# Keys and queries of the last three batches: turned by blocked loads and VectorE copies instead of TensorE

## The chip, the cores and the metric

The kernel runs on one core of a Trainium2 chip, as a single program in a single launch. The metric is the device time of one execution in microseconds, and less is better. Instructions stand in one queue for each engine and run there in that order: TensorE (PE; its weight loads are PEld) multiplies matrices into PSUM, VectorE (DVE) and ScalarE (ACT) work elementwise on SBUF and PSUM, GpSimd (POOL) masks, clears and takes maxima over partitions, and SyncE (SP) issues nearly all DMAs. An instruction waits at the head of its queue until what it needs is there, and what is queued behind it waits too.

## What is computed

Attention with decay over 4 batches, 8 heads, 576 tokens and a head size of 64, and after it two feed-forward layers over all 2304 tokens, everything in float32:

```python
scores = scale * np.matmul(q, k.transpose(0, 1, 3, 2))
log_f = np.log(np.clip(f, 0.0001, 1.0))
cum = np.cumsum(log_f, axis=-1)
scores = np.where(causal, -1e9, scores + cum[:, :, :, None] - cum[:, :, None, :])
attn = softmax(scores)                                 # over the keys
x = (attn @ v), heads side by side: [2304, 512]
h = x @ moe_w_in;    x = (np.maximum(h, 0) + alpha * np.minimum(h, 0)) @ moe_w_out
h = x @ moe2_w_in;   out = np.where(h >= 1, h, np.where(h <= -1, 0, (h + 1) ** 2 / 4)) @ moe2_w_out
```

`w_in` is 512 by 2048 and `w_out` 2048 by 512 in both layers.

## The kernel before

**Order.** The kernel is written as a list of tasks. `add(engine, duration, function, position, dependencies, ...)` puts one on the list, and `Order.emit` walks through time with the durations and latencies that the source states, takes for each engine the ready task with the lowest position, and calls its function, which records the instructions. That fixes each engine's queue when the program is built; the hardware then only follows it. `Ring` and `Buf` are the planner's buffers: a task that takes a new buffer waits until all users of its previous content are done. A change in one task's engine or stated duration therefore moves tasks all over the queues.

**Precision.** Large products are made of three matmuls: a float32 value is split into a leading part (`...hi`, a copy to the type float32r, on ScalarE) and a remainder (`...lo`, a subtraction, on VectorE), and the small by small product is left out.

**Stages.** The first batch's attention (`plain_pair`, the units `u < 2`) runs in about the first 100 us. The other three batches follow, 24 units of work: three batches, two row blocks each (256 rows, then 320), four head pairs each. Between their tasks stand those of the first feed-forward layer (`l1_slice`: twelve matmuls of 256 columns into `ps_h` in L1320, the activation in L1330 to L1343, and twelve into `ps_y` in L1359), in chunks of 256 tokens. From about 480 us on the rest of the first layer and the whole second layer follow.

**One unit of the last three batches** (L831 to L1197). `load_k` and `load_q` fetch the pair's keys and queries with `load_tok`: token on the partition, the two heads' 2 x 64 values beside each other in a row, 256 bytes a run, one DMA for each head and one more for the last 64 tokens of a block of 320. They land in a `raw` buffer (two of them, shared with V) and in `qr` (one). Scores need the head size on the partitions, so `ktr` (L881) and `qtr` (L918) turn them on TensorE, 128 tokens a matmul, into a PSUM buffer of the ring `s` (three buffers, which the scores use too). From there `khi` (L892) and `klo` (L895) write leading part and remainder of the keys to `kT`, on either half of the partitions for the pair's two heads, and `qhi`, `qhi2`, `qlo` (L928, L935, L931) do so for the queries; with that, one matmul of 128 partitions makes two of the three partial products. Keys of the first 256 tokens are kept in DRAM (`stash`, L905) and read again (`reload`, L871) for the second row block, so that it turns only the remaining 320, as three groups of 128 with padding.

Behind that come the score matmuls (L994), bias and mask (L1008, L545), the maximum over the keys (L1029, L1047, L1053), the exponential (L1069, L1074), its split (L1084, L1088), the product with V (L1108 to L1116), and the division by way of two small DMA trips (`gather`, `put`, `get`: L1154 to L1175).

## Time and profile before

| | us |
|---|---|
| median of three runs | 1004.61 |
| the three runs | 1007.04, 1003.51, 1004.61 |
| the profiled execution's own time | 1004.37 |
| its span | 1002.2 |
| TensorE busy in the span | 987.8 |
| VectorE busy | 773.3 |
| ScalarE busy | 628.6 |
| GpSimd busy | 111.1 |

The profile is that of one execution. The span runs from its first instruction to its last; 2.2 us lie outside of it. An engine's busy time counts from an instruction's start to its end, overlaps once. Instructions of one engine overlap: a matmul of 256 columns lasts 286 ns by the page, though the next one begins well before. What one takes in its queue is therefore read from one start to the next in the timeline. "L881" is a line of the kernel before. A releaser ("<- DVE g L1333") is what ended a wait.

### The profile page before, as it was taken

How to read it: one execution, taken by the hardware profiler on the slowest of the kernel's cores; microseconds unless marked ns; L12 is line 12 of the kernel's file. 1: busy time of each engine (PE TensorE's matmuls, PEld its weight loads, DVE VectorE, ACT ScalarE, POOL GpSimd, SP SyncE). 2: the span in 40 equal slices, each digit the busy share in tenths (PEclk: the TensorE clock that was granted, in tenths of full speed). 3: DMA queues.
4: the chain of work that ended last, by engine and by line, in shares of the span. 5: the costliest groups of instructions: out<-in, count | busy, mean ns of one | idle time of the engine just before them, and what ended most of it. 6: DMA issues, size and time to landing. Idle time of an engine off the chain costs nothing.

```text
span 1002.2 us, 19921 instructions
## 1 busy us (share of the span) xinstructions
PE 987.8 (99%) x6736; PEld 909.2 (91%) x6736; DVE 773.3 (77%) x1874; ACT 628.6 (63%) x1628; POOL 111.1 (11%) x222
## 2 busy tenths in 40 slices
...
GB/s 264 232 184 156 63 76 100 55 74 56 63 109 55 62 55 76 106 45 31 29 92 192 183 203 242 116 316 237 268 102 249 153 123 120 116 168 125 106 53 63
DMA packets 151940, 128.24 MB, mean 128 GB/s; under 512 B 83440, under 2 KB 122368, under 8 KB 151840
## 3 DMA queue, kind: packets, MB, share of 16 engines
...
q10 hardware_dynamic: 1088, 0.26, 0.1%
...
## 4 chain that ended last, share of the span: by engine, by line
PE 80%; DVE 10%; ACT 5%; issue 2%; DMA 2%; POOL 0%; SPq 0%; ACTq 0%; POOLq 0%
PE ps_z L1598 20%; PE ps_y L1359 12%; PE ps_h L1854 12%; PE ps_h L1320 12%; PE ps_h L1613 7%; PE ps_y L1447 4%; PE ps_h L1403 4%; PE ps_s L994 3%; DVE raw L1253 1%; PE ps_o L1108 1%; DVE raw L1258 1%; PE ps_o L1114 1%; PE ps_o L1116 1%; PE ps_o L1115 1%; DVE w L1272 1%
## 5 line engine op out<-in xcount | busy, mean ns | idle before, releaser
L1320 PE MATMUL ps_h<-x,w 128*128 128x256 f32 x1344 | 182.7, 286 | 1.9 <-DVE g L1333 1.6
L1359 PE MATMUL ps_y<-gg,w 128*128 128x256 f32 x1344 | 183.5, 286 | 0.0
L1320 PEld LDWEIGHTS ps_h<-x,w 128*128 128x128 f32 x1344 | 168.7, 190 | 3.0 <-DVE g L1333 2.4
L1359 PEld LDWEIGHTS ps_y<-gg,w 128*128 128x128 f32 x1344 | 168.9, 190 | 0.4
L1598 PE MATMUL ps_z<-w,gw 128*128 128x512 f32 x576 | 149.2, 393 | 0.0
L1854 PE MATMUL ps_h<-xc,wc 128*128 128x384 f32 x672 | 136.8, 338 | 0.0
L1854 PEld LDWEIGHTS ps_h<-xc,wc 128*128 128x128 f32 x672 | 121.2, 188 | 10.3
L1598 PEld LDWEIGHTS ps_z<-w,gw 128*128 128x128 f32 x576 | 106.7, 188 | 15.3
L1892 ACT ACTIVATE t<-t,half 128x384 f32<-128x384 f32 x64 | 39.5, 617 | 88.6 <-DVE t L1889 88.6
L1008 ACT ACTIVATE S<-ps_s,nb 128x320 f32<-128x320 f32 (+4 forms) x168 | 75.2, 453 | 10.0 <-PE ps_s L994 5.9
L1333 DVE SCALAR_TENSOR_TENSOR g<-g,calpha,ps_h 128x256 f32<-128x256 f32 x112 | 53.4, 478 | 30.8 <-ACT g L1330 29.2
L1598 PE MATMUL ps_z<-w,gg 128*128 128x512 f32 x288 | 72.4, 391 | 0.0
L994 PE MATMUL ps_s<-q,kT 128*128 128x320 f32 (+4 forms) x336 | 72.0, 297 | 0.4 <-ACT S L1008 0.3
L1901 ACT CAST gw<-t 128x384 fp32r<-128x384 f32 x64 | 32.6, 510 | 56.9 <-PE ps_z L1598 54.1
L1074 ACT ACTIVATE S<-S 128x320 f32<-128x320 f32 (+2 forms) x144 | 59.8, 425 | 11.0 <-DVE S L1069 10.6
L545 POOL TENSOR_SCALAR_AFFINE_SELECT S<-S 128x128 f32<-128x128 f32 (+1 forms) x120 | 41.4, 347 | 223.4 <-ACT S L1008 209.4
L1904 DVE TENSOR_TENSOR gw<-t,gw 128x384 fp32r<-128x384 f32 x64 | 35.5, 555 | 37.6 <-ACT gw L1901 36.8
L1053 POOL PARTITION_ALL_REDUCE pp<-pp x48 | 57.3, 1194 | 52.2 <-DVE pp L1047 22.9
L1330 ACT ACTIVATE g<-ps_h 128x256 f32<-128x256 f32 x112 | 42.8, 382 | 32.0 <-PE ps_h L1320 31.1
L1069 DVE TENSOR_TENSOR S<-pp,S 128x320 f32<-128x320 f32 (+4 forms) x168 | 57.9, 396 | 5.1 <-POOL pp L1053 4.7
L1598 PEld LDWEIGHTS ps_z<-w,gg 128*128 128x128 f32 x288 | 53.0, 188 | 9.5
L1342 DVE TENSOR_TENSOR gg<-g,gg 128x256 fp32r<-128x256 f32 x112 | 48.5, 433 | 12.7 <-ACT gg L1339 11.0
...
## 6 DMA issues: line engine op xcount, KB each, us to landing
wc<-wc SPq DMA_DIRECT2D x112, 256.0 KB, 2.7
...
```

The lines of the kernel that those rows point to most:

```text
L994: nc.tensor.matmul(out=sb.t[:, :m], lhsT=kt.t[:, kb * P:(kb + 1) * P], rhs=qt.t[:, t * NMAX + qo:t * NMAX + qo + m], start=(t == 0), stop= ...
L1008: nc.scalar.activation(out=Sb.t[:, so:so + m], in_=sb.t[:, :m], func=AF.Identity, bias=bias)
L1053: nc.gpsimd.partition_all_reduce(Mb.t[:, :n], Mx.t[:, :n], P, ReduceOp.max)
L1069: nc.vector.tensor_tensor(out=sl, in0=Mb.t[:, qo:qo + m], in1=sl, op=ALU.subtract)
L1074: nc.scalar.activation(out=Sb.t[:, :gn], in_=Sb.t[:, :gn], func=AF.Exp, scale=-SCALE)
L1320: nc.tensor.matmul(out=hb.t, lhsT=a[:, sl], rhs=b, start=(cc == 0 and t == 0), stop=(cc == NCC - 1 and t == 2))
L1333: nc.vector.scalar_tensor_tensor(out=gb.t, in0=gb.t, scalar=calpha[:, s:s + 1], in1=hb.t, op0=ALU.mult, op1=ALU.add)
L1342: nc.vector.tensor_tensor(out=gg.t[1], in0=gb.t, in1=gg.t[0].bitcast(F32), op=ALU.subtract)
L1359: nc.tensor.matmul(out=Y[c][e // 2][:, e % 2, :], lhsT=a[:, sl], rhs=b, start=(s == 0 and t == 0 and e % 2 == 0), stop=(s == NF - 1 and t ...
L1598: nc.tensor.matmul(out=zb.t, lhsT=a, rhs=b, start=(start and t == 0), stop=(stop and t == 2))
L1613: nc.tensor.matmul(out=hb.t, lhsT=a[:, sl], rhs=b, start=(cc == 0 and t == 0), stop=(cc == NCC - 1 and t == 2))
L1854: nc.tensor.matmul(out=hb.t[:, :m], lhsT=wb.t[:, z, sl], rhs=xb.t[y][:, cc, :], start=(begin and cc == 0 and t == 0), stop=(cc == 1 and t ...
```

## The change

A DMA places squares of 32 by 32 values. `load_blocks` makes four DMAs of a load, one for each head and each half of its 64 values; each fills 32 partitions. Token 32 i + r of a block goes to partition r of its quarter, and its 32 values to columns 32 i to 32 i + 31, so every run is 128 bytes. One copy of VectorE (`nc.vector.transpose`, a STREAM_TRANSPOSE over 128 partitions) then turns each square in its place, from the first 320 columns of the same buffer to the next 320, and what results is what `ktr` and `qtr` left in PSUM: head size on the partitions, tokens on the columns. The splits read it from there, from SBUF and not from PSUM. No PSUM buffer is taken, and the buffers of the loads are held until the last split is done. Keys are turned without padding, 320 columns for 384, and a memset of GpSimd (`kpad`) clears the 64 padded columns of `kT` in the units of 320 rows. `qr` grows from three blocks of 128 to five. The first batch's `plain_pair` and the loads of V stay as they were. The counts in the queues: 120 matmuls fewer, 48 copies more on VectorE, 24 memsets more on GpSimd, 192 DMAs of the new form for 120 of the old.

```diff
--- before.py
+++ after.py
@@ -218,6 +218,7 @@
     BH = B * H
     C1 = 256
     NRAW = 3
+    Z = 32
     NVAL = 10
     QA = 256
     RC = 3
@@ -457,11 +458,11 @@
         return A1[nm]
 
     RAW = [ap2.tile([P, NKB, 2, D], F32, name=f"raw{i}") for i in range(2)]
-    QR = [ap1.tile([P, 3, 2, D], F32, name="qr")]
+    QR = [ap1.tile([P, NKB, 2, D], F32, name="qr")]
     pads(V["vF"])
     for t in RAW:
         nc.gpsimd.memset(t[S % P:, NKB - 1], 0.0)
-    nc.gpsimd.memset(QR[0][S % P:, 2:], 0.0)
+    nc.gpsimd.memset(QR[0][S % P:, 2:3], 0.0)
     nc.gpsimd.memset(ph["qr"][S % P:, 2:], 0.0)
 
     def load_tok(dst, src, b, pr, t0, t1, eng=nc.sync):
@@ -477,6 +478,16 @@
                 out=dst[:r, n, :, :],
                 in_=src[b, 2 * pr:2 * pr + 2, t0 + n * P:t1, :].rearrange("h p d -> p h d"))
 
+
+    def load_blocks(dst, src, b, pr, t0, t1):
+        for j in range(2):
+            for x in range(0, D, Z):
+                nc.sync.dma_start(
+                    out=dst[j * D + x:j * D + x + Z, :t1 - t0].rearrange("r (i c) -> r i c", c=Z),
+                    in_=src[b, 2 * pr + j, t0:t1, x:x + Z].rearrange("(i r) c -> r i c", r=Z))
+
+    def flat(t):
+        return t.rearrange("p c j d -> p (c j d)")
 
     fb = {}
     fP = Buf(R["s"])
@@ -837,17 +848,17 @@
         k0 = QA if again else 0
 
         def load_k(kb_=kb_, b=b, pr=pr, nk=nk, k0=k0):
-            kb_.t = RAW[kb_.slot]
-            load_tok(kb_.t[:, k0 // P:], k, b, pr, k0, nk)
+            kb_.t = flat(RAW[kb_.slot])
+            load_blocks(kb_.t, k, b, pr, k0, nk)
 
         def load_q(qb_=qb_, b=b, pr=pr, q0=q0, q1=q1):
-            qb_.t = QR[0]
-            load_tok(qb_.t, q, b, pr, q0, q1)
-
-        T["lk"] = add("SP", tok_issue(k0, nk), load_k, p0 - 3, [last.get("lv"), last.get("lk")], new=[kb_],
-                      move=moved(2 * (nk - k0), 256))
+            qb_.t = flat(QR[0])
+            load_blocks(qb_.t, q, b, pr, q0, q1)
+
+        T["lk"] = add("SP", 1900, load_k, p0 - 3, [last.get("lv"), last.get("lk")], new=[kb_],
+                      move=moved(4 * (nk - k0), 128))
         last["lk"] = T["lk"]
-        last["lq"] = add("SP", tok_issue(q0, q1), load_q, p0 - 3, [last.get("lq")], new=[qb_], move=moved(2 * n, 256))
+        last["lq"] = add("SP", 1900, load_q, p0 - 3, [last.get("lq")], new=[qb_], move=moved(4 * n, 128))
 
         nsplit = sum(y[2] > PVF for y in blocks)
         nkp = -(-nk // P) * P
@@ -871,32 +882,30 @@
                     nc.sync.dma_start(out=k_of(j).bitcast(F32)[:, :QA], in_=kd[j])
 
                 kready[j].append(add("SP", 450, reload, p0 - 1, [owned[j]] + keep_st[b, pr], use=[kx[j]], move=moved(P, 4 * QA)))
-        for t0 in range(k0, nkp, KC):
-            t1 = min(nkp, t0 + KC)
-            pb = Buf(R["s"])
-
-            def ktr(pb=pb, kb_=kb_, t0=t0, t1=t1):
-                pb.t = ps_a.tile([P, 512], F32, tag=f"s{pb.slot}", name="pst")
-                for c in range(t0 // P, t1 // P):
-                    nc.tensor.transpose(
-                        pb.t[:, c * P - t0:(c + 1) * P - t0],
-                        kb_.t[:, c, :, :].rearrange("p j d -> p (j d)"), ident)
-
-            a = last["ktr"] = add("PE", 112 * (t1 - t0) // P, ktr, p0 - 1, [T["lk"], last.get("ktr"), owned[0]],
-                                  new=[pb], use=[kb_])
-            for j in range(2):
-                hr = slice(j * D, (j + 1) * D)
-                lr = slice(D - j * D, 2 * D - j * D)
-
-                def khi(j=j, hr=hr, pb=pb, t0=t0, t1=t1, k_of=k_of):
-                    nc.scalar.copy(out=k_of(j)[hr, t0:t1], in_=pb.t[hr, :t1 - t0])
-
-                def klo(j=j, hr=hr, lr=lr, pb=pb, t0=t0, t1=t1, k_of=k_of):
-                    nc.vector.tensor_tensor(out=k_of(j)[lr, t0:t1], in0=pb.t[hr, :t1 - t0],
-                                            in1=k_of(j)[hr, t0:t1].bitcast(F32), op=ALU.subtract)
-
-                h = add("ACT", act(t1 - t0), khi, p0 - 1 + j * JO, [a, owned[j]], use=[pb, kx[j]])
-                kready[j] += [h, add("DVE", dve(t1 - t0), klo, p0 - 1 + j * JO, [h], use=[pb, kx[j]])]
+        nl = nk - k0
+
+        def ktr(kb_=kb_, nl=nl):
+            nc.vector.transpose(out=kb_.t[:, GMAX:GMAX + nl], in_=kb_.t[:, :nl])
+
+        a = last["ktr"] = add("DVE", dve(nl), ktr, p0 - 1, [T["lk"], last.get("ktr")], use=[kb_])
+        for j in range(2):
+            hr = slice(j * D, (j + 1) * D)
+            lr = slice(D - j * D, 2 * D - j * D)
+            if nk < nkp:
+                def kpad(j=j, k_of=k_of, nk=nk, nkp=nkp):
+                    nc.gpsimd.memset(k_of(j).bitcast(F32)[:, nk:nkp], 0.0)
+
+                kready[j].append(add("POOL", 230, kpad, p0 - 1, [owned[j]], use=[kx[j]]))
+
+            def khi(j=j, hr=hr, kb_=kb_, nl=nl, k_of=k_of, k0=k0, nk=nk):
+                nc.scalar.copy(out=k_of(j)[hr, k0:nk], in_=kb_.t[hr, GMAX:GMAX + nl])
+
+            def klo(j=j, hr=hr, lr=lr, kb_=kb_, nl=nl, k_of=k_of, k0=k0, nk=nk):
+                nc.vector.tensor_tensor(out=k_of(j)[lr, k0:nk], in0=kb_.t[hr, GMAX:GMAX + nl],
+                                        in1=k_of(j)[hr, k0:nk].bitcast(F32), op=ALU.subtract)
+
+            h = add("ACT", act(nl), khi, p0 - 1 + j * JO, [a, owned[j]], use=[kb_, kx[j]])
+            kready[j] += [h, add("DVE", dve(nl), klo, p0 - 1 + j * JO, [h], use=[kb_, kx[j]])]
         if not again and nk == QA:
             kept[b, pr] = tc.dram_tile([2, P, QA], F32, name=f"kept{b}_{pr}")
             keep_st[b, pr] = []
@@ -907,36 +916,31 @@
                 keep_st[b, pr].append(add("SP", 450, stash, p0 + 1, kready[j], use=[kx[j]], move=moved(P, 4 * QA)))
 
         qready = [[], []]
-        pb = Buf(R["s"])
         qx = [Buf(R[f"qp{j}"]) for j in range(2)]
-        np_ = -(-n // P)
-
-        def qtr(pb=pb, qb_=qb_, np_=np_, qx=qx):
-            pb.t = ps_a.tile([P, 512], F32, tag=f"s{pb.slot}", name="pst")
-            qx[0].t = second("q0")
-            for c in range(np_):
-                nc.tensor.transpose(pb.t[:, c * P:(c + 1) * P], qb_.t[:, c].rearrange("p j d -> p (j d)"), ident)
+
+        def qtr(qb_=qb_, n=n):
+            nc.vector.transpose(out=qb_.t[:, GMAX:GMAX + n], in_=qb_.t[:, :n])
 
         pq = p0 + QOFF
-        a = add("PE", 112 * np_, qtr, pq, [last["lq"], last.get("qtr")] + plain_qk[0] + plain_qk[1], new=[pb, qx[0]], use=[qb_])
+        a = add("DVE", dve(n), qtr, pq, [last["lq"], last.get("qtr")] + plain_qk[0] + plain_qk[1], use=[qb_])
         last["qtr"] = a
         for j in range(2):
             hr = slice(j * D, (j + 1) * D)
 
-            def qhi(pb=pb, qb=qx[j], n=n, hr=hr, j=j):
+            def qhi(qb_=qb_, qb=qx[j], n=n, hr=hr, j=j):
                 qb.t = second(f"q{j}")
-                nc.scalar.copy(out=qb.t[hr, :n], in_=pb.t[hr, :n])
-
-            def qlo(pb=pb, qb=qx[j], n=n, hr=hr):
-                nc.vector.tensor_tensor(out=qb.t[hr, NMAX:NMAX + n], in0=pb.t[hr, :n], in1=qb.t[hr, :n].bitcast(F32),
+                nc.scalar.copy(out=qb.t[hr, :n], in_=qb_.t[hr, GMAX:GMAX + n])
+
+            def qlo(qb_=qb_, qb=qx[j], n=n, hr=hr):
+                nc.vector.tensor_tensor(out=qb.t[hr, NMAX:NMAX + n], in0=qb_.t[hr, GMAX:GMAX + n], in1=qb.t[hr, :n].bitcast(F32),
                                         op=ALU.subtract)
 
-            def qhi2(pb=pb, qb=qx[j], n=n, hr=hr, lr=slice(D - j * D, 2 * D - j * D)):
-                nc.scalar.copy(out=qb.t[lr, :n], in_=pb.t[hr, :n])
-
-            h = add("ACT", act(n), qhi, pq + j * JO, [a], new=[qx[j]] if j else [], use=[pb] if j else [pb, qx[j]])
-            h2 = add("ACT", act(n), qhi2, pq + j * JO, [a, h], use=[pb, qx[j]])
-            qready[j] = [h, h2, add("DVE", dve(n), qlo, pq + j * JO, [h], use=[pb, qx[j]])]
+            def qhi2(qb_=qb_, qb=qx[j], n=n, hr=hr, lr=slice(D - j * D, 2 * D - j * D)):
+                nc.scalar.copy(out=qb.t[lr, :n], in_=qb_.t[hr, GMAX:GMAX + n])
+
+            h = add("ACT", act(n), qhi, pq + j * JO, [a], new=[qx[j]], use=[qb_])
+            h2 = add("ACT", act(n), qhi2, pq + j * JO, [a, h], use=[qb_, qx[j]])
+            qready[j] = [h, h2, add("DVE", dve(n), qlo, pq + j * JO, [h], use=[qb_, qx[j]])]
 
         vb_ = Buf(R["raw"])
```

The order moves everywhere from the first of these units on. Three places, each from the kernel before and from the changed one, whose file is four lines longer by then (its L998 is L994, L1118 is L1114, L1324 is L1320, L1363 is L1359). TensorE's queue in the second batch, second row block, in the scores (`ps_s`) of a pair's second head; before:

```order
L1320 MATMUL ps_h<-x,w 128x256 x12
L994 MATMUL ps_s<-q_1911,kT 128x320 x2
L881 MATMUL pst<-ident,raw_163 128x128 x3
L994 MATMUL ps_s<-q_1911,kT 128x320 x2
L1114 MATMUL ps_o<-PH,vH 128x320
L1115 MATMUL ps_o<-PH,vL 128x320
L1116 MATMUL ps_o<-PL,vH 128x320
L994 MATMUL ps_s<-q_1911,kT 128x320 x2
```

The changed kernel at the scores of the second head there:

```order
L998 MATMUL ps_s<-q_1975,kT 128x320 x2
L1363 MATMUL ps_y_3415<-gg,w 128x256 x6
L1363 MATMUL ps_y_3416<-gg,w 128x256 x6
L998 MATMUL ps_s<-q_1975,kT 128x320 x2
L1118 MATMUL ps_o<-PH,vH 128x320
L1119 MATMUL ps_o<-PH,vL 128x320
L1120 MATMUL ps_o<-PL,vH 128x320
L998 MATMUL ps_s<-q_1975,kT 128x320 x2
```

The three transposing matmuls between two score matmuls are gone, and other wide groups stand between the scores.

VectorE's queue near the same place, where the remainders of keys (L895) and queries (L931) stand between passes of the softmax (L1047, L1088) and of the feed-forward layer (L1333, L1342); before:

```order
L1342 TENSOR_TENSOR gg<-g,gg 128x256
L1047 TENSOR_TENSOR pp<-S,pp 128x320
L895 TENSOR_TENSOR kT<-pst,kT 64x384
L1088 TENSOR_TENSOR PL<-S,PH 128x320
L931 TENSOR_TENSOR q_1858<-pst,q_1858 64x320
L1047 TENSOR_TENSOR pp<-S,pp 128x192
L1333 SCALAR_TENSOR_TENSOR g<-g,calpha,ps_h 128x256 x2
L895 TENSOR_TENSOR kT<-pst,kT 64x384
L1088 TENSOR_TENSOR PL<-S,PH 128x320
```

The changed kernel, with the copies (L888 for keys, L922 for queries) and the remainders (L904, L935):

```order
L1051 TENSOR_TENSOR pp<-S,pp 128x64
L1092 TENSOR_TENSOR PL<-S,PH 128x320
L888 STREAM_TRANSPOSE raw_164<-raw_164 128x320
L904 TENSOR_TENSOR kT<-raw_164,kT 64x320
L1073 TENSOR_TENSOR S<-pp,S 128x320
L1092 TENSOR_TENSOR PL<-S,PH 128x320
L1073 TENSOR_TENSOR S<-pp,S 128x320 x2
L1073 TENSOR_TENSOR S<-pp,S 128x192
L1073 TENSOR_TENSOR S<-pp,S 128x64
L1033 TENSOR_TENSOR pp<-S 128x320
L1337 SCALAR_TENSOR_TENSOR g<-g,calpha,ps_h 128x256
```

The copies are new rows in this queue, and the remainders read `raw` and `qr` where they read `pst`, the PSUM buffer.

SyncE's queue of the second batch, the key load of the first unit of 320 rows; before:

```order
L471 DMA raw_164<-in_k_dram 128x2x64 x2
L476 DMA raw_164<-in_k_dram 64x2x64
L1165 DMA m_2403<-spread_1_175 64x256
L1165 DMA pp<-spread_1_175 64x256
L471 DMA qr<-in_q_dram 128x2x64 x2
L476 DMA qr<-in_q_dram 64x2x64
```

The changed kernel at the same load:

```order
L485 DMA raw_164<-in_k_dram 32x10x32 x4
L485 DMA qr<-in_q_dram 32x10x32 x4
L1169 DMA m_2430<-spread_1_175 64x256
L1169 DMA pp<-spread_1_175 64x256
```

Three DMAs for the keys became four, and the four of the queries now stand right behind them, ahead of the small DMAs of the division (`m`, `pp`).

## Rows read from the trace of the kernel before

**Rows 1.** Page, part 1: busy us (share of span), instructions.

```profile
PE 987.8 (99%) x6736; PEld 909.2 (91%) x6736; DVE 773.3 (77%) x1874; ACT 628.6 (63%) x1628; POOL 111.1 (11%) x222
```

**Rows 2.** Windows: us; busy PE, PEld, DVE, ACT, POOL; PEclk, DMA share, GB/s.

```profile
100.00:480.00 380.00, 376.39 (x3102) 370.50 (x3100) 311.02 (x839) 315.37 (x925) 96.32 (x167) 1.00 0.28 69
...
520.00:600.00 80.00, 80.00 (x384) 67.48 (x383) 75.77 (x169) 47.01 (x108) 0.00 (x0) 1.00 0.65 196
...
600.00:1002.00 402.00, 398.45 (x1985) 351.52 (x1983) 273.14 (x588) 164.69 (x336) 0.00 (x0) 1.00 0.52 160
```

**Rows 3.** Timeline of TensorE: start us, us, line, operation, shape, count.

```profile
151.48 0.38 PE L881 MATMUL pst<-ident,raw 128*128 128x128 f32 x2
151.62 1.67 PE L1359 MATMUL ps_y<-gg,w 128*128 128x256 f32 x12
...
161.81 0.49 PE L881 MATMUL pst<-ident,raw 128*128 128x128 f32 x3
162.06 1.67 PE L1359 MATMUL ps_y<-gg,w 128*128 128x256 f32 x12
163.56 0.28 PE L1114 MATMUL ps_o<-PH,vH 128*128 128x256 f32 x1
...
163.92 1.59 PE L1359 MATMUL ps_y<-gg,w 128*128 128x256 f32 x12
165.34 0.38 PE L1108 MATMUL ps_o<-S,vF 128*128 128x128 f32 x2
```

**Rows 4.** One line, TensorE: ns min/median/max, first and last start.

```profile
L881 PE MATMUL pst<-ident,raw x60: 270/272/300, 110.2 to 460.3; 128*128 128x128 f32 x60
```

**Rows 5.** Timeline of VectorE: back-to-back passes.

```profile
160.28 0.71 DVE L1069 TENSOR_TENSOR S<-pp,S 128x256 f32<-128x256 f32 x2
160.91 0.28 DVE L1029 TENSOR_TENSOR pp<-S 128x128 f32<-128x128 f32 x1
...
179.22 0.48 DVE L931 TENSOR_TENSOR q<-pst,q 64x320 fp32r<-64x320 f32 x1
179.62 0.47 DVE L1088 TENSOR_TENSOR PL<-S,PH 128x320 fp32r<-128x320 f32 x1
```

**Rows 6.** Groups by shape, 100 to 480 us: busy us, mean ns.

```profile
L1069 DVE TENSOR_TENSOR S<-pp,S 128x320 f32<-128x320 f32 x69 | 30.2, 485 | 3.3 <-POOL pp L1053 3.0
L895 DVE TENSOR_TENSOR kT<-pst,kT 64x384 fp32r<-64x384 f32 x24 | 13.3, 556 | 2.3 <-ACT kT L892 1.5
L931 DVE TENSOR_TENSOR q<-pst,q 64x320 fp32r<-64x320 f32 x24 | 11.7, 486 | 1.5 <-ACT q L935 0.7 <-ACT q L928 0.4
...
L1245 DVE TENSOR_SCALAR val<-val 128x512 int32<-128x512 int32 x6 | 2.5, 425 | 0.0
...
L1339 ACT CAST gg<-g 128x256 fp32r<-128x256 f32 x88 | 35.7, 408 | 9.4 <-DVE g L1333 8.5
...
L928 ACT CAST q<-pst 64x256 fp32r<-64x256 f32 x24 | 8.8, 366 | 0.2
```

**Rows 7.** Two lines of VectorE, columns as in rows 4.

```profile
L1342 DVE TENSOR_TENSOR gg<-g,gg x112: 395/424/954, 45.2 to 526.4; 128x256 fp32r<-128x256 f32 x112
...
L931 DVE TENSOR_TENSOR q<-pst,q x48: 409/452/496, 122.9 to 467.0; 64x256 fp32r<-64x256 f32 x24, 64x320 fp32r<-64x320 f32 x24
```

**Rows 8.** TensorE waits, 100 to 480 us: total us, times, longest.

```profile
PE ps_h L1320 <- DVE g L1333: 1.6, 4, 0.6
PE pst L881 <- DMA raw<-in_k_dram: 0.5, 1, 0.5
```

**Rows 9.** SyncE timeline; DMA issues: KB each, median us to landing.

```profile
156.53 0.96 SPq L471 DMA_DIRECT2D raw<-in_k_dram  x2
157.54 0.64 SPq L476 DMA_DIRECT2D raw<-in_k_dram  x1
...
raw<-in_k_dram SPq DMA_DIRECT2D x54, 64.0 KB, 2.5
```

**Rows 10.** Groups by shape, 100 to 480 us, GpSimd.

```profile
L414 POOL MEMSET vH<- 128x192 f32 x1 | 0.3, 263 | 19.1 <-PE ps_o L746 19.1
```

## The prediction, made before the changed kernel had run

> **What bounds the kernel now.** I read the page first, for the engine that fills the span: TensorE is busy 987.8 us, 99% of the span [rows 1]. [...] Attention of the last three batches lies at about 100 to 480 us; there TensorE is busy 376.39 of 380.00 us, so it idles 3.6 us in all, while VectorE is busy 311.02 (idle 69.0), ScalarE 315.37 (idle 64.6) and GpSimd 96.32 [rows 2]. From 600 us to the end it idles 3.6 of 402 us. So the time is the length of TensorE's queue: a column less in it shortens the run, as long as no other engine makes it wait. Then I read the timeline of TensorE for what one of the removed groups takes from start to start, since its busy times overlap.
>
> **What goes from TensorE.** The 120 transposing matmuls stand in 48 groups: each of 24 units of work (three batches, two row blocks, four head pairs) has one group for keys and one for queries, of two matmuls in the 12 units of 256 rows and of three in the 12 of 320. That is 24 groups of two and 24 of three; the row of one line shows its half, x60 [rows 4]. A group of two holds the queue from 151.48 to 151.62, 0.14 us; one of three from 161.81 to 162.06, 0.25 us [rows 3]. So 24 x 0.14 + 24 x 0.25 = 9.4 us.
>
> There is a second part. The twelve matmuls of 256 columns behind a group of three take 162.06 to 163.56, 1.50 us, and behind a wide matmul 163.92 to 165.34, 1.42 us [rows 3]: what follows a narrow matmul starts its successor 0.08 us later. In the old order 102 matmuls of 256 columns or more stand behind one of 128 or fewer, 41 of them behind a transposing group; in the new order 64 do. So 38 x 0.08 = 3.0 us. Together TensorE's queue loses **12.4 us**, between 9.4 (if the second part stays) and 12.4.
>
> **What VectorE gets.** 48 transposing copies, 24 of 128x256 and 24 of 128x320. No row shows such a copy. Bounds: a pass of two inputs goes from start to start in 0.32 us at 256 columns (two from 160.28 to 160.91, 0.63) and 0.40 at 320 (179.22 to 179.62) [rows 5]. A pass with one input over 512 columns takes 425 ns [rows 6], against some 0.69 that two-input passes of that width would take at 556 ns per 384 plus 1.1 ns a column, so 0.6 of it: 0.20 and 0.25. Above, a copy that goes at half rate costs two passes, 0.64 and 0.80. So 24 x (0.20 + 0.25) = 10.8, 24 x (0.32 + 0.40) = 17.3, or 24 x (0.64 + 0.80) = 34.6 us. I take the middle: the copy reads each column once and writes it once, which is what the one-pass rows do. Against that, the subtraction for the keys' remainder covers 320 columns in place of 384 in the 12 larger units, once for each of two heads: 24 passes go from 556 to the 486 ns that the queries' 320 columns take [rows 6], 1.7 us. Net +15.6 us (9.1 to 32.9), of 69.0 idle.
>
> The 96 subtractions now read their first input from SBUF and not from PSUM. At 320 columns a pass whose inputs both lie in SBUF takes 485 ns on the mean, and the queries' subtraction from PSUM 486 [rows 6]: no difference, so I price it at nothing. [...]
>
> **ScalarE, GpSimd, SyncE.** ScalarE's 144 splits read SBUF: at 256 columns 408 ns from SBUF against 366 from PSUM [rows 6], so 144 x 0.042 = 6.0 us, in 64.6 of idle; the shorter key rows give about 1 us of it back. GpSimd gets 24 memsets of 128x64; one of 128x192 took 263 ns [rows 10], so at most 6.3 us in 284 of idle. SyncE issues four DMAs for a load: it was 0.96 us for two, and 0.64 for the third one of a 320-row load [rows 9]. At 0.48 a piece a load takes 1.92 (0.96 more for 256 rows, 0.32 more for 320), at 0.64 a piece 2.56: 48 loads make 31 to 61 us of issue time in a stage of 380. What is queued behind is the denominators' round trip, the next V and the weights. A load of 64 KB lands 2.5 us after its issue in the median [rows 9]. No row shows one in runs of 128 bytes, as they are now; if each of its four DMAs took as long and they overlap, as the issues do, it lands one to two issues later. Loads are asked for three positions ahead of their first use, and TensorE waited for one once, 0.5 us [rows 8]. So I put SyncE at nothing, 0 to 8 us (rival 3).
>
> **The wait that is added.** VectorE now waits for a load itself (four landings) before a transposing copy, and ScalarE and VectorE then wait for that copy. Behind a waiting copy stand the passes of the softmax and the feed-forward's remainder, for which TensorE waits: the feed-forward's matmul behind its activation already makes up 1.6 us of TensorE's waits [rows 8]. TensorE's own cover is its order: between those waits it has groups of twelve matmuls, 1.42 us each [rows 3]. I allow new stalls as long as the whole stage has now, rounded down: **3.0 us**, with 0 below (a PSUM buffer that the groups held is free for scores) and the whole 12.4 above.
>
> **Sum.** The profiled run took 1004.37 us, 0.24 under the median 1004.61, so a difference carries over. 1004.6 - 12.4 + 3.0 = **995.2 us**.
>
> **Rivals.**
>
> 1. *VectorE becomes the bound: slower.* With 15.6 more, VectorE works 326.6 us in the stage, which is to be 367.6 long: its waits would have to shrink from 69.0 to 41.0 us. If they stay above 53.4 nothing is gained (326.6 + 53.4 = 380). Halfway between that and no shrinking at all, 61 us, the stage is 387.8 long and the time 1004.6 + 7.8 = 1012. It decides sooner if the copy goes at half rate: then VectorE works 343.9, and 36 us of waits are the limit. Against it: between 520 and 600 us VectorE is busy 75.77 of 80.00 with TensorE at 80.00 [rows 2], so an order made ahead can run both full. For it: in this stage its waits are largely on ScalarE and GpSimd in chains, and the change makes the chain of a load longer by one link in this queue: 9 of the 48 copies have at most one pass behind them before the remainder that needs ScalarE's split of that copy, 0.37 us at 256 columns [rows 6], so VectorE stands still there. Chance 0.12.
>
> 2. *GpSimd holds the new subtractions: no change.* The pass with both inputs in SBUF has a longest of 954 ns against a median of 424, while the subtraction from PSUM never passes 496 [rows 7]. If each unit's last subtraction ahead of the scores is held by those 0.53 us and TensorE waits it out, 24 x 0.53 = 12.7 us eat the gain: 1004.9. Against it: the long one is rare; its median stays within 29 ns of its least, 395. [...] Chance 0.06.
>
> 3. *Loads come late: most of the gain is lost.* If the copies wait for the longer issue, 0.32 us a unit for keys or queries, and TensorE waits that out in each of the 24, it costs 7.7 us more: 1004.6 - 12.4 + 3.0 + 7.7 = 1002.9. For it: TensorE has met one late key load [rows 8]. Against it: loads are asked for early. Chance 0.08.
>
> That the change doesn't do what it says is left out: in the new order the 120 matmuls are gone and the 48 copies stand there.
>
> **How the numbers follow.** Forecast 0.74, rivals 0.12, 0.06 and 0.08. A difference under 0.3%, 3.0 us, can't be told from none. The forecast's own range runs from 990.5 (the 12.4 and half of the 3.6 us of stalls gone too) to 1001.6; to hold 8 in 10, rival 3 belongs in it: 990.5 to 1003.5 leaves out rivals 1 and 2 and a little at the low end. Faster is the forecast, 0.74; within 0.3% rivals 2 and 3, 0.14; slower rival 1, 0.12.
>
> **What would show it.** Right: TensorE's instructions fall by 120, its stage ends some 9 us sooner, all later stages keep their length, TensorE's idle time in the stage is 4 to 8 us, and a copy of 320 columns takes 0.4 us from start to start. Wrong: copies of 0.7 us or more; waits of the score matmuls or of the feed-forward's matmuls for VectorE beyond 10 us in total (rival 1 if VectorE is busy over 92%, rival 2 if single subtractions of over 0.7 us end just ahead of them); or idle time of VectorE ahead of the copies that the loads end (rival 3). A stage that is 9 us shorter and a later one that is longer would refute that the time is TensorE's queue.

## The result: 0.6% slower where a gain was forecast

| | before | after |
|---|---|---|
| median, us | 1004.67 (1003.43 to 1007.04) | 1011.18 (1010.84 to 1012.01) |
| the profiled execution's own time, us | 1004.37 | 1010.84 |
| its span, us | 1002.2 | 1009.0 |
| first matmul of the part behind the stage (L1403, now L1407), us | 525.9 | 532.2 |
| last matmul's end, us | 998.4 | 1004.7 |

The ratio is 1.0062, 95% interval 1.0051 to 1.0073, so the change costs 5.1 to 7.3 us. I had forecast 995.2 us and a range up to 1003.5. Nearly all of the loss lies ahead of the part that follows the attention: that part begins 6.3 us later, and from there to the end it is 472.5 us in both kernels.

Lines of the changed kernel are four higher than before in this part (L1320 is L1324). The page, busy time and its share, and the granted clock in 40 slices:

```profile
PE 984.5 (98%) x6616; PEld 900.2 (89%) x6616; DVE 790.1 (78%) x1922; ACT 634.0 (63%) x1628; POOL 116.4 (12%) x246
PEclk9999999999989999999999999999999999999999
```

The windows of after, for comparison with [rows 2]; behind the stretch and its length stand the busy times of PE, PEld, DVE, ACT and POOL with the number of instructions, then the granted clock, the DMA share and GB/s:

```profile
100.00:480.00 380.00, 366.67 (x2932) 355.23 (x2931) 324.50 (x878) 317.34 (x916) 103.12 (x192) 0.99 0.31 68
480.00:600.00 120.00, 120.00 (x735) 108.59 (x734) 92.68 (x214) 65.86 (x160) 2.02 (x4) 1.00 0.45 133
600.00:1000.00 400.00, 400.00 (x1993) 353.18 (x1992) 277.09 (x599) 166.15 (x340) 0.00 (x0) 1.00 0.53 160
```

In 100 to 480 us TensorE now idles 13.3 us, where it idled 3.6 [rows 2]; VectorE works 13.5 us more and is still at 85%. The 120 matmuls are gone from TensorE's queue, and its waits took their place. TensorE's waits in that stretch by what ended them (total us, times, longest us), for [rows 8]:

```profile
PE ps_h L1324 <- DVE g L1337: 4.7, 2, 4.0
PE ps_o L1120 <- DVE PL L1092: 2.5, 6, 1.4
PE ps_o L1118 <- ACT PH L1088: 2.2, 4, 1.3
PE ps_y L1363 <- DVE gg L1346: 1.0, 3, 0.5
```

One wait stands out, 4.0 us. The chain that ended last, in order of time (start, us, what), around it:

```profile
270.59 0.44 SPq L485
...
274.07 2.14 DMA pp<-spread
276.24 0.46 DVE raw L888
...
278.88 0.42 DVE qr L922
279.30 0.32 DVE pp L1179
...
279.85 0.29 ACT x L1189
280.14 0.37 ACT S L1012
...
283.61 0.46 ACT q L932
284.10 0.30 DVE q L935
...
284.71 0.62 DVE S L1073 x2
...
285.54 0.40 DVE g L1337
285.98 2.93 PE ps_h L1324 x12
```

Read downward: SyncE issues eight DMAs of keys and queries and only then the denominators' way back (`pp<-spread`); VectorE works through both new copies (L888, L922) before it takes what that trip brought (L1179); ScalarE splits the result (L1189) and has a dozen more instructions to do before it comes to the layer's activation (L1334, in front of L1337), whose matmuls were done at about 278 us. The last line is twelve matmuls of 256 columns in 2.93 us from the first one's start to the last one's end, where twelve took 1.59 before [rows 3]. The windows say why:

```profile
276.00:282.00 6.00, 5.54 (x45) 5.14 (x44) 4.55 (x15) 3.55 (x11) 0.67 (x3) 1.00 0.42 123
282.00:285.98 3.98, 0.00 (x0) 0.00 (x0) 2.67 (x8) 3.77 (x13) 1.89 (x6) 0.92 0.46 108
285.98:292.16 6.18, 6.18 (x29) 6.18 (x30) 5.43 (x17) 3.98 (x13) 1.01 (x1) 0.50 0.57 129
292.16:298.00 5.84, 5.84 (x50) 5.84 (x49) 2.89 (x7) 3.59 (x11) 0.58 (x2) 1.00 0.38 66
```

In the 3.98 us that TensorE stands still ScalarE is busy 3.77: at that place it is ScalarE's queue that is full. Right behind it TensorE's clock is granted at 0.50 for 6.18 us. In the profiled execution of the kernel before, the clock in the stage never fell (1.00) [rows 2].

**The books.** Busy time hides waits: a matmul of 256 columns counts 286 ns, though its successor starts 118 ns after it (twelve in 1.42 us [rows 3]). So I counted on TensorE's timeline, from 100 us to the first matmul of L1403, each time from one start to the next, less 0.417 ns for each of the first one's columns, less 12 ns. That makes 119 ns at 256 columns and 225 at 512; the kernel before shows 119 (twelve from 528.61 to 530.04 us) and 228 (24 from 530.04 to 535.51). What stays over 100 ns is a wait. What a matmul takes more in a stretch at half clock (213 ns from start to start at 256 columns, in the changed kernel behind 285.98 us) is counted apart. Each row is one execution, the profiled one.

| kernel | end of the stage, us | waits, us | half clock, us | waits and half clock against before | the rest against before |
|---|---|---|---|---|---|
| before | 525.9 | 14.6 | 0 | | |
| after | 532.2 | 31.1 | 2.9 | +19.4 | -13.1 |

The rest, 6.3 - 19.4 = -13.1 us, is what left the queue; I had put it at 12.4. New waits and half clock are 19.4; I had put them at 3.0. Of them 10.1 us are waits over 0.4 us (17 against 10), 1.9 lie between 0.18 and 0.4, and 4.5 between 0.1 and 0.18 us.

### The profile page after: what moved, and what is told of

The parts are those of the page before. It is cut to its first block, busy times and chain, and to the rows that moved or that the text cites. A ratio compares the mean times of both kernels' runs of the same rounds, so it can differ in the third digit from the quotient of the medians.

```text
span 1009.0 us, 19855 instructions
## 1 busy us (share of the span) xinstructions
PE 984.5 (98%) x6616; PEld 900.2 (89%) x6616; DVE 790.1 (78%) x1922; ACT 634.0 (63%) x1628; POOL 116.4 (12%) x246
## 4 chain that ended last, share of the span: by engine, by line
PE 71%; DVE 11%; ACT 7%; issue 4%; DMA 3%; SPq 2%; POOL 1%; DVEq 0%; ACTq 0%; POOLq 0%
PE ps_z L1602 20%; PE ps_h L1858 12%; PE ps_y L1363 8%; PE ps_h L1324 8%; PE ps_h L1617 7%; PE ps_y L1451 4%; PE ps_h L1407 4%; SPq L485 2%; PE ps_s L998 2%; ACT S L1012 1%; PE ps_s L663 1%; DMA pp<-spread 1%; DVE S L1073 1%; DVE raw L1257 1%; PE ps_o L1112 1%
## 5 line engine op out<-in xcount | busy, mean ns | idle before, releaser
L1324 PE MATMUL ps_h<-x,w 128*128 128x256 f32 x1344 | 183.5, 286 | 5.9 <-DVE g L1337 4.7
L1363 PE MATMUL ps_y<-gg,w 128*128 128x256 f32 x1344 | 183.9, 286 | 1.1 <-DVE gg L1346 1.0
L1324 PEld LDWEIGHTS ps_h<-x,w 128*128 128x128 f32 x1344 | 169.9, 192 | 7.1 <-DVE g L1337 5.3
L1363 PEld LDWEIGHTS ps_y<-gg,w 128*128 128x128 f32 x1344 | 170.5, 192 | 2.4 <-DVE gg L1346 2.1
L1337 DVE SCALAR_TENSOR_TENSOR g<-g,calpha,ps_h 128x256 f32<-128x256 f32 x112 | 52.7, 475 | 26.3 <-ACT g L1334 25.6
L998 PE MATMUL ps_s<-q,kT 128*128 128x320 f32 (+4 forms) x336 | 71.2, 296 | 0.6 <-ACT S L1012 0.3
L1057 POOL PARTITION_ALL_REDUCE pp<-pp x48 | 59.2, 1234 | 57.7 <-DVE pp L1051 26.2
L1334 ACT ACTIVATE g<-ps_h 128x256 f32<-128x256 f32 x112 | 42.3, 379 | 24.7 <-PE ps_h L1324 24.0
```

Source lines behind the costliest of these rows:

```text
L998: nc.tensor.matmul(out=sb.t[:, :m], lhsT=kt.t[:, kb * P:(kb + 1) * P], rhs=qt.t[:, t * NMAX + qo:t * NMAX + qo + m], start=(t == 0), stop= ...
L1057: nc.gpsimd.partition_all_reduce(Mb.t[:, :n], Mx.t[:, :n], P, ReduceOp.max)
L1324: nc.tensor.matmul(out=hb.t, lhsT=a[:, sl], rhs=b, start=(cc == 0 and t == 0), stop=(cc == NCC - 1 and t == 2))
L1337: nc.vector.scalar_tensor_tensor(out=gb.t, in0=gb.t, scalar=calpha[:, s:s + 1], in1=hb.t, op0=ALU.mult, op1=ALU.add)
L1363: nc.tensor.matmul(out=Y[c][e // 2][:, e % 2, :], lhsT=a[:, sl], rhs=b, start=(s == 0 and t == 0 and e % 2 == 0), stop=(s == NF - 1 and t ...
```

## Experiments: what the two new links cost

Theory 1 is SyncE (longer issue), theory 2 VectorE (copies), theory 3 the order that the planner made.

**Old loads in the new order.**

```diff
-            load_blocks(kb_.t, k, b, pr, k0, nk)
+            load_tok(RAW[kb_.slot], k, b, pr, k0, nk)
-            load_blocks(qb_.t, q, b, pr, q0, q1)
+            load_tok(QR[0], q, b, pr, q0, q1)
```

> The changed kernel in its own order, but keys and queries are fetched again by the two or three DMAs of the old form (so what VectorE turns is no longer keys and queries, and the output is not attention); copies, splits and the place of every instruction stay. SyncE's issue time falls from about 1.9 us for a load to 0.96 (256 rows) or 1.60 (320 rows). Theory 1 (SyncE: eight load issues in a row delay the trip of the denominators, and through the queues of ScalarE and VectorE TensorE): the stalls that the changed kernel has more than the one before, 13.3 - 3.6 = 9.7 us in 100 to 480 us, and the 3.4 us of half clock behind the longest go for the most part: 1011.2 - 9.7 - 3.4 = 998, or at least 1004. Theory 2 (VectorE: 16.8 us more work and one link more in its queue): no change, 1011 within 1.5. Theory 3 (the stalls lie in the order that the planner made, whatever the single durations): a small gain, 1008 to 1011, and the 4.0 us stall at 286 us stays.

Measured: 1007.98 us, ratio to before 1.0024 (1.0011 to 1.0038), against 1.0062 for the whole change. The new form of the loads costs 3 to 4 us. SyncE's timeline (start, us) shows how much longer it takes to issue them; first the changed kernel, then this one (what the loads' landing adds, the run does not separate):

```profile
270.15 1.87 SPq L485 DMA_DIRECT2D raw<-in_k_dram  x4
272.07 1.96 SPq L485 DMA_DIRECT2D qr<-in_q_dram  x4
274.07 1.11 SPq L1169 DMA_DIRECT2D pp<-spread  x2
```

```profile
268.99 0.90 SPq L472 DMA_DIRECT2D raw<-in_k_dram  x2
269.93 0.98 SPq L472 DMA_DIRECT2D qr<-in_q_dram  x2
271.01 0.65 SPq L477 DMA_DIRECT2D qr<-in_q_dram  x1
271.76 1.19 SPq L1169 DMA_DIRECT2D pp<-spread  x2
```

From the first load to the denominators' issue it is 2.8 us and not 3.9. Yet the long stall stays: 4.3 us from start to start at 284.6, with 0.50 of the clock behind it. Theory 1 explains a part and not the long stall, though the chain above runs through the issues.

**Narrow copies in the new order.** The first try cleared the load buffers ahead of the first loads, and its first 60 us show the harm: TensorE busy 45.25 us there, against 53.12 in the changed kernel. The keys' copy is shown, the queries' is narrowed in the same way:

```diff
-            nc.vector.transpose(out=kb_.t[:, GMAX:GMAX + nl], in_=kb_.t[:, :nl])
+            nc.vector.transpose(out=kb_.t[:, GMAX:GMAX + Z], in_=kb_.t[:, :Z])
...
+    for t in RAW + QR:
+        nc.gpsimd.memset(t, 0.0)
```

> The changed kernel in its own order and with its own loads, but each of the 48 copies of VectorE turns 32 columns and not 256 or 320 (the splits read what an earlier content left, so the output is not attention). VectorE gets about 48 x 0.25 = 12 us back, the rest of the 17 us that the copies take from start to start. Theory 1 (SyncE): 1011 within 1.5. Theory 2 (VectorE): most of the 9.7 us of new stalls and the half clock behind them go, 1000, at least 1005. Theory 3 (the order): 1008 to 1011, with the 4.0 us stall at 286 us still there.

```profile
0.00:60.00 60.00, 45.25 (x429) 39.07 (x430) 45.10 (x118) 42.24 (x112) 10.57 (x38) 1.00 0.76 220
```

It took 1018.75 us, and says nothing on the copies but by the stage itself, 361.5 us from the first score matmul to the last against 362.8. The run with both edits had the same fault (1014.49 us):

> Both edits at once in the order of the changed kernel: old loads and copies of 32 columns (the output is not attention). What is left against the kernel before is the 120 transposing matmuls gone, ScalarE's slightly longer reads from SBUF, and the other order. Theories 1 and 2 together: what I forecast without any new stall, 1004.6 - 12.4 = 992, up to 997. Theory 3 (the order itself holds the stalls): 1004 to 1008, since the 4.0 us stall and the half clock behind it stay and only small waits go.

Both again, with full width in the few copies that first fill a buffer (the keys' lines; the queries' are alike):

```diff
+            w = nl if full_for.get(kb_.slot, 0) < nl else Z
+            full_for[kb_.slot] = max(nl, full_for.get(kb_.slot, 0))
+            nc.vector.transpose(out=kb_.t[:, GMAX:GMAX + w], in_=kb_.t[:, :w])
```

> The narrow copies once more, without what disturbed the first try (clearing the load buffers at the start held the first loads up by 9 us): a copy has its full width where its buffer was not yet filled that far, in the first few units, and 32 columns in all others, some 43 of the 48 (the output is not attention). In the first try the time from the first score matmul to the last was 361.5 us against 362.8 in the changed kernel. Theory 2 (VectorE's load), by the 8.0 us that the same copies cost in the order of the kernel before: 1011.2 - 8 = 1003. Theory 3 (the order holds the stalls): 1011.2 - 1.3 = 1010, with the stall of 4 us near 286 us still there.

> The changed kernel in its own order with both edits, old loads and copies of 32 columns (full width only where a buffer was not yet filled that far; the output is not attention). Singly they took 3.2 us (loads) and 1.7 to 2.8 us (copies) off. If the two costs are separate they add up: 1011.2 - 3.2 - 2.3 = 1005.7. If either link alone holds the same waits, the second edit adds nothing: 1007 to 1008. Theory 3 (order): not below 1004 in any case, since the long stall and the half clock, 7.4 us, are in the order.

In both, 42 of the 48 copies are narrow, and such a copy still takes an estimated 0.2 us (from the 438 ns at 256 columns and 502 at 320 of the keys' copies in the changed kernel, 1.0 ns a column). Copies alone: 1.0035 (1.0023 to 1.0048), so 2.7 us off. With the old loads too: 1.0017 (1.0000 to 1.0034), 4.5 us off, where 3.8 for the loads and 2.7 for the copies make 6.5; the intervals are too wide to tell whether the two add up. It is most of what was lost against before, but nowhere near the forecast: with neither the longer issue nor most of the copies' length, TensorE has 120 matmuls fewer and the time is that of before or 0.3% above it. The stall at 284 us is in both.

**The copies in the old order.** More copies, TensorE's turns kept; the first two lines stand in `klo`, the others in `qlo`, ahead of the subtraction:

```diff
+                    if j == 0 and t0 == k0:
+                        nc.vector.transpose(out=TW[:, :w], in_=TW[:, :w])
...
+                if j == 0:
+                    nc.vector.transpose(out=TW[:, :n], in_=TW[:, :n])
```

> The kernel before with its order and loads, and 48 more transposing copies of VectorE of the same widths (on a tile that nobody else uses), each straight ahead of the first remainder of a unit's keys or queries. It is the load on VectorE alone, 17 us, with TensorE's transposing matmuls kept. Theory 1 (SyncE) and theory 3 (order): 1004.7, up to 1007. Theory 2 (VectorE): the copies push TensorE by as much as the changed kernel lost against its own sum, 6.5 + 12.4 = 19 us at the most, at least 8: 1012 to 1023.

Measured: 1013.74 us, ratio 1.0085 (1.0062 to 1.0108), at the low end of theory 2. But it is 36 copies and not 48: those for the keys in the 12 units of 256 rows were not made, since `klo` reads `k0` only when the order is built, and by then it is 256 for all units. The copies that the trace has:

```profile
L936 DVE STREAM_TRANSPOSE tw<-tw 128x320 f32<-128x320 f32 x12 | 6.0, 504 | 0.0
L898 DVE STREAM_TRANSPOSE tw<-tw 128x320 f32<-128x320 f32 x12 | 6.0, 500 | 0.0
L936 DVE STREAM_TRANSPOSE tw<-tw 128x256 f32<-128x256 f32 x12 | 5.3, 439 | 0.1
```

The window, against [rows 2]:

```profile
100.00:480.00 380.00, 372.65 (x3048) 364.28 (x3048) 319.24 (x862) 311.03 (x913) 95.12 (x164) 1.00 0.27 68
```

VectorE works 8.2 us more there (786.6 - 773.3 = 13.3 us over the whole run, since the stage is longer) and has 61 us left, and still TensorE idles 7.4 us and not 3.6. So 36 copies, 13.3 us of busy time, cost about 8 us, and VectorE's free 69 us [rows 2] were not free: of an instruction put into its queue, a good part is passed on to TensorE. What the other 12 copies would have added is not shown.

## Experiments: is the stage as long as TensorE's queue?

This is the premise on which my sum stood. First try: leave the turns out of the kernel before and let the splits read the load (the keys' lines; the queries' are alike).

```diff
-                pb.t = ps_a.tile([P, 512], F32, tag=f"s{pb.slot}", name="pst")
-                for c in range(t0 // P, t1 // P):
-                    nc.tensor.transpose(
-                        pb.t[:, c * P - t0:(c + 1) * P - t0],
-                        kb_.t[:, c, :, :].rearrange("p j d -> p (j d)"), ident)
+                pb.t = kb_.t.rearrange("p c j d -> p (c j d)")[:, t0:]
```

> The kernel before with its order and its loads, but the 120 transposing matmuls are left out and the splits read what the load brought (so the scores are not those of keys and queries). Nothing is put in their place on VectorE or SyncE; only ScalarE's 144 splits read SBUF, 5 to 6 us more of its work. It is TensorE's gain alone, in the old order. Theory 4 (the stage is as long as TensorE's queue, as the prediction had it): 1004.7 - 9.4 = 995.3 to 1004.7 - 12.4 = 992.3. Theory 5 (chains through the other engines set the stage's length nearly as much as TensorE does, so that idle time takes the place of a part of the removed matmuls): 997 to 1002, with TensorE's idle time in 100 to 480 us grown from 3.6 to between 6 and 10 us.

Measured: 1073.66 us, ratio 1.067. No theory had that. The splits now hold the load buffers, in an order made for buffers that a turn had freed. The waits of VectorE in 60 to 520 us:

```profile
DVE q L925 <- DMA qr<-in_q_dram: 26.4, 10, 4.3
```

Ten of the queries' remainders wait for loads, 26.4 us in all. In this order the later release of the load buffers cost far more than the turns take; in the changed kernel the planner knew of it.

Second try, shown against the first: the splits read a tile that nobody writes.

```diff
-                pb.t = kb_.t.rearrange("p c j d -> p (c j d)")[:, t0:]
+                pb.t = TW
```

> TensorE's gain alone once more, without what spoiled the first try (there the splits read the load buffers and so held them: 67 us). The kernel before with its order and its loads; the 120 transposing matmuls are left out, and the splits read a constant tile that nobody writes (so the scores are not those of keys and queries, and nobody waits for these loads). Theory 4 (the stage is as long as TensorE's queue): 1004.7 - 9.4 = 995.3 to 1004.7 - 12.4 = 992.3. Theory 5 (chains through the other engines set the length nearly as much): 997 to 1002, and TensorE's idle time in 100 to 480 us grows from 3.6 to 6 us and more.

Measured: 1006.89 us, beside 1005.33 for the kernel before in the same series; ratio **1.0000 (0.9986 to 1.0014)**. The matmuls are gone, no instruction is put in their place, and the time stays. Window and TensorE's waits:

```profile
100.00:480.00 380.00, 369.64 (x2967) 358.80 (x2966) 312.07 (x834) 318.34 (x924) 98.72 (x167) 1.00 0.27 67
```

```profile
PE ps_h L1316 <- DVE g L1329: 3.9, 4, 2.0
PE ps_s L990 <- ACT S L1004: 1.7, 6, 0.4
PE ps_o L1110 <- ACT pp L1138: 1.2, 2, 0.7
PE ps_s L990 <- DMA kT<-kept: 1.0, 2, 0.6
PE ps_o L1112 <- DVE PL L1084: 0.7, 3, 0.3
```

TensorE's idle time is 10.4 us for 3.6; the waits are small ones on ScalarE, VectorE and a DMA alike. Theory 4 falls; even theory 5 had hoped for 3 us.

One thing besides the matmuls did change: the splits read SBUF and not PSUM, as in the changed kernel, and take longer on the mean. On the page VectorE is busy 776.0 us for 773.3 and ScalarE 632.5 for 628.6. Two of the groups, for 366 ns (the same width) and 486 ns [rows 6]:

```profile
L890 ACT CAST kT<-tw 64x256 fp32r<-64x256 f32 x24 | 9.7, 403 | 1.1 <-PE ps_s L990 0.9
L927 DVE TENSOR_TENSOR q<-tw,q 64x320 fp32r<-64x320 f32 x24 | 12.5, 522 | 0.8 <-ACT q L924 0.5
```

No run separates what these few us cost. They don't save the premise: if the time were the length of TensorE's queue, work on engines that idle 62 to 68 us in this window would not have shown. Is it the old order? The planner told that a turn takes 1 ns:

```diff
-            a = last["ktr"] = add("PE", 112 * (t1 - t0) // P, ktr, p0 - 1, [T["lk"], last.get("ktr"), owned[0]],
+            a = last["ktr"] = add("PE", 1, ktr, p0 - 1, [T["lk"], last.get("ktr"), owned[0]],
-        a = add("PE", 112 * np_, qtr, pq, [last["lq"], last.get("qtr")] + plain_qk[0] + plain_qk[1], new=[pb, qx[0]], use=[qb_])
+        a = add("PE", 1, qtr, pq, [last["lq"], last.get("qtr")] + plain_qk[0] + plain_qk[1], new=[pb, qx[0]], use=[qb_])
```

> As the run that left the turns out and read a constant tile (1.0000 of the kernel before), but the planner is told that a turn takes 1 ns, so that it makes an order for TensorE without them. Theory 4b (the gain is there, the old order kept it from showing): 1004.7 - 12.4 = 992, up to 998. Theory 5 (another chain is about as long as TensorE's queue, so idle time takes the place of the turns in any order): 1001 to 1006, with stalls in 100 to 480 us of 8 us and more.

Measured: 1004.64 us, ratio 0.9983 (0.9970 to 0.9996). An order of its own gives 0.4 to 3 us, not 12, and TensorE idles 11.2 us in 100 to 480 us. Theory 5 fits, in the one order that was run.

**Is VectorE the second bound?** Shorten some of its work in the old order, with the turns and without (`short` gives 32 where the buffer was filled before):

```diff
-                nc.vector.tensor_tensor(out=qb.t[hr, NMAX:NMAX + n], in0=pb.t[hr, :n], in1=qb.t[hr, :n].bitcast(F32),
+                w = short(n, f"q{j}", 0, n)
+                nc.vector.tensor_tensor(out=qb.t[hr, NMAX:NMAX + w], in0=pb.t[hr, :w], in1=qb.t[hr, :w].bitcast(F32),
-                    nc.vector.tensor_tensor(out=mo, in0=Sb.t[:, so:so + m], in1=mo, op=ALU.max)
+                    nc.vector.tensor_tensor(out=mo[:, :32], in0=Sb.t[:, so:so + 32], in1=mo[:, :32], op=ALU.max)
```

> The kernel before with its order and its turns; VectorE's work is shortened: 44 of the 48 subtractions for the queries' remainder and 64 of the 72 later maxima over a unit's key blocks do 32 columns and not all (so remainders and maxima are partly wrong). By their pitch of 0.32 to 0.40 us and some 0.27 us this takes about 44 x 0.25 + 64 x 0.17 = 22 us off VectorE. Theory 4 (TensorE's queue is the only bound): 1004.7, at the best its 3.6 us of idle time, 1001. Theory 5 (TensorE and the chains through VectorE are equally long): also 1001 to 1004.7, since TensorE's queue is still there.

> The same shorter VectorE work, and the 120 transposing matmuls left out as well (splits read a constant tile). Without the turns alone it was 1.0000 of the kernel before. Theory 5 (two bounds): now both are shorter, and TensorE's 12.4 us show for the most part: 992 to 998. If VectorE has no part in it (the second bound is ScalarE, GpSimd or the DMA trips): 1001 to 1005 as without the turns alone.

Measured, ratios to the kernel before:

| | VectorE as it was | VectorE shorter |
|---|---|---|
| with turns | 1 | 0.9972 (0.9960 to 0.9985) |
| without turns | 1.0000 (0.9986 to 1.0014) | 0.9949 (0.9933 to 0.9965) |

The windows, with turns and then without:

```profile
100.00:480.00 380.00, 376.77 (x3121) 372.28 (x3121) 292.83 (x843) 317.56 (x932) 94.42 (x167) 1.00 0.29 69
```

```profile
100.00:480.00 380.00, 371.86 (x3018) 363.28 (x3017) 295.16 (x846) 323.06 (x937) 95.49 (x170) 1.00 0.28 69
```

The pair gains 5.1 us, the single ones 2.8 and 0: some of TensorE's matmuls show once VectorE has 18 us less to do, but only about 2 of 12. The rest is still filled with waits, 8.1 us of idle time in this window, though VectorE idles 85 us and ScalarE 57. So the load of TensorE and VectorE alone is not what sets the time. What fits is chains that go through VectorE, ScalarE, GpSimd and the DMA trips, each with its turn in a queue. That is argued and not shown: no run here shortened ScalarE's, GpSimd's or the trips' part, and which link is the next one stays open.

The books for these kernels, counted as above (the profiled execution of "turns out, old order" took 1007.17 us, that of the kernel before 1004.37, so their ends lie further apart than the ratio says):

| kernel | end of the stage, us | waits, us | half clock, us | waits and half clock against before | the rest against before |
|---|---|---|---|---|---|
| 36 copies added, turns kept | 532.9 | 21.1 | 0 | +6.5 | +0.5 |
| turns out, old order | 528.9 | 27.1 | 1.5 | +14.0 | -11.0 |
| turns out, own order | 527.1 | 26.2 | 1.4 | +13.0 | -11.8 |
| VectorE shorter | 523.6 | 12.4 | 0 | -2.2 | -0.1 |
| VectorE shorter, turns out | 521.4 | 22.2 | 0 | +7.6 | -12.1 |
| key buffer (below) | 528.0 | 29.4 | 0 | +14.8 | -12.7 |

Wherever the turns are gone, 11 to 13 us have left TensorE's queue, and 8 to 19 us of waits have come, the changed kernel included.

## Experiments: how much of it is the order

The planner makes a new order whenever a task changes. Constants of it, with the same work:

```diff
-SLACK = 100
+SLACK = 150
-    RATE = 31
+    RATE = 31.5
-    QOFF = 0
+    QOFF = 0.5
```

> The changed kernel, whole, with three constants of the planner changed: the margin that it keeps ahead of TensorE's waits 150 ns and not 100, the pace of the first layer's chunks 31.5 and not 31, the queries' position half a step later. Work, loads and copies are the same; the order is another. Theory 3 (order): the 4.0 us stall and the 3.4 us at half clock behind it go, and small waits with the wider margin: 1011.2 - 7.4 = 1003.8, or a little lower, 1000. Theories 1 and 2 (the work of SyncE and VectorE costs the time, wherever it stands): 1011 within 2.

> The control: the kernel before with the same three constants. It has no stall of over 0.9 us to lose. Theory 3 (order): within 3 us of 1004.7 in either direction, so that the changed kernel's gain from the same constants is due to its long stall. If the constants help whatever the kernel, it gains as much as the changed one, some 7 us.

The changed kernel took 1.0020 (1.0009 to 1.0031) of before, 4.2 us less than in its first order; the kernel before with the same constants 1.0008 (0.9998 to 1.0018). Singly, first the margin:

```diff
-SLACK = 100
+SLACK = 150
```

> The changed kernel, whole, with one constant of the planner changed: the margin ahead of TensorE's waits 150 ns and not 100. Theory 3 (the order made the difference): each order of this work has stalls of its own at other places, and the times scatter by some 4 us around the three seen so far with this work and these buffers (1011.2, 1008.1): 1004 to 1012. Theory 6 (the buffers that hold the loads cost the time in any order): 1008 to 1012, never at the 1004.9 of the kernel with the key buffer.

and then the queries' position:

```diff
-    QOFF = 0
+    QOFF = -1
```

> The changed kernel, whole, with one other constant changed: the queries' copy and splits one position sooner. Theory 3 (order): 1004 to 1012. Theory 6 (buffers): 1008 to 1012.

Measured: 1.0035 (1.0021 to 1.0050) and 1.0002 (0.9990 to 1.0014). So four orders of the changed kernel lie at 1.0062, 1.0035, 1.0020 and 1.0002: the first one is the worst of them, and the best is as long as the kernel before. Of the kernel before only one other order was run, so how far its own orders scatter is not known. The stall of 4 us belongs to the first order, and it stays there when loads and copies are shortened. The orders at 1.0035 and 1.0020 have one of 1.9 and of 2.0 us at 170 us, with the clock at 0.50 behind it (on the mean of 150 to 200 us it is 0.97 in the second); in the profiled execution of the order at 1.0002 no wait is over 1.2 us, and the clock is 1.00 in the whole stage.

**A buffer of their own for the keys.** Copies in place make room for it (main lines; the queries are turned in place too):

```diff
+    KRT = [ap2.tile([P, GMAX], F32, name=f"kr{i}") for i in range(KR)]
-            kb_.t = flat(RAW[kb_.slot])
+            kb_.t = KRT[kb_.slot]
-            nc.vector.transpose(out=kb_.t[:, GMAX:GMAX + nl], in_=kb_.t[:, :nl])
+            nc.vector.transpose(out=kb_.t[:, :nl], in_=kb_.t[:, :nl])
```

> The changed kernel, whole, with a buffer of their own for the keys of the last three batches, so that the two buffers they shared with V are V's alone; to make room the copies turn each square in place, which halves what a load takes. The planner's constants stay, and it makes a new order. Theory 6 (a load's buffer is now held until the last split has read it, where TensorE's turn had freed it before; so loads start late, stand in SyncE's queue in a bunch, and hold up the denominators' trip behind them): the 4.0 us stall near 286 us, the 3.4 us at half clock and a part of the small waits go: 1011.2 - 7.4 = 1003.8, to 1000. If the bunch of eight issues only moves elsewhere, or VectorE's load is what costs: 1008 to 1012.

```diff
-SLACK = 100
+SLACK = 170
-    QOFF = 0
+    QOFF = -1
```

> The same with two constants of the planner changed: the margin ahead of TensorE's waits 170 ns and not 100, the queries' work one position sooner. Theory 3 (order, on top of theory 6): small waits go as well, 1 to 3 us below the run with the key buffer alone, 998 to 1003, which would be below the kernel before. If the order matters little once loads come in time: within 1 us of the run with the key buffer alone.

```diff
-SLACK = 100
+SLACK = 170
-    RATE = 31
+    RATE = 31.5
-    QOFF = 0
+    QOFF = -0.5
```

> The kernel with the key buffer in a third order (margin 170 ns, pace 31.5, queries half a position sooner). The two orders before it took 0.9985 and 1.0021 of the kernel before. Theory 3 (order): anywhere from 1003 to 1009. Theory 6 (buffers): below the orders of the changed kernel without that buffer on the mean of the three, that is at 1007 or less.

Three orders: 0.9985 (0.9970 to 1.0000), 1.0021 (1.0006 to 1.0036) and 0.9985 (0.9974 to 0.9996). The mean is 0.9997, that of the four without the buffer 1.0030: 3 us in favour of the buffer, with orders that scatter as much. The second run, where I expected a gain from the wider margin, was 3.6 us worse than the first. That the buffer helps is likely and not shown. The best of these, 1004.93 us beside 1006.49 for the kernel before in the same series, is ahead of both kernels, by 0.15% against the one before: less than the 0.3% that I called the limit of what can be told.

## Why the prediction was wrong, point by point

**"The time is the length of TensorE's queue: a column less in it shortens the run, as long as no other engine makes it wait."** This is the step that failed. I read it from a busy share of 99% and 3.6 us of idle time [rows 1, 2]. Busy time counts each matmul to its end, 286 ns for a pitch of 118, and so hid most of the 14.6 us of waits of the count above; and little idle time tells that TensorE is hardly waiting now, not that nothing else is as long. With the turns out and no instruction added, the time stayed within 0.14% in the old order and fell by 1.7 us in one of its own. TensorE's busy share was no good measure here: it is 98% in the kernels without the turns and was 99% with them, for 11 to 13 us less of matmuls and hardly a gain in time.

**Term: "I allow new stalls as long as the whole stage has now, rounded down: 3.0".** It measured 19.4 us. In the run that only leaves the turns out there are 14.0 already; the remaining 5 to 6 go with loads, copies and order together, and the runs don't split them further. My upper bound was the whole 12.4, which only brings the time back to that of before; nothing in my sum let the waits grow past the work removed.

**Term: TensorE's queue, -12.4.** Right: -13.1, the follow-on part included.

**Term: VectorE, +15.6.** Right in size, 790.1 - 773.3 = +16.8. The groups of the copies and of the subtractions from SBUF in the changed kernel (count, busy us, mean ns, idle time before):

```profile
L922 DVE STREAM_TRANSPOSE qr<-qr 128x320 f32<-128x320 f32 x12 | 6.1, 508 | 1.6 <-DMA qr<-in_q_dram 1.6
L922 DVE STREAM_TRANSPOSE qr<-qr 128x256 f32<-128x256 f32 x12 | 5.3, 439 | 0.2
L888 DVE STREAM_TRANSPOSE raw<-raw 128x256 f32<-128x256 f32 x12 | 5.3, 438 | 0.6 <-DMA raw<-in_k_dram 0.5
L904 DVE TENSOR_TENSOR kT<-raw,kT 64x320 fp32r<-64x320 f32 x24 | 12.7, 530 | 3.2 <-ACT kT L901 2.6
L935 DVE TENSOR_TENSOR q<-qr,q 64x320 fp32r<-64x320 f32 x24 | 12.4, 518 | 3.0 <-ACT q L932 2.4
```

A copy took 0.37 us at 256 columns and 0.43 at 320 from start to start where the next pass followed at once; I had reckoned with 0.32 and 0.40. But I priced it at nothing because 69 us were idle. In the old order 36 such copies cost about 8 us.

**The subtractions, at nothing.** Nearly: 518 ns on the mean from SBUF at 320 columns against 486 from PSUM [rows 6], but 489 in the median against 488.5, so the mean is longer by a few long ones (rival 2 below); the 530 of the keys at 320 columns are more than the 486 that I had put there, so the 1.7 us that I took off VectorE for the padding did not come in full.

**ScalarE, +5.** Right: 634.0 - 628.6 = 5.4. It, too, is no free engine where it counts: in the 4 us stall it is busy 95%.

**SyncE, 31 to 61 us of issue at nothing.** The lower end fits the loads shown, 1.87 and 1.96 us for four DMAs; the price of nothing does not, since the loads cost 3 to 4 us in the changed order, within my range of 0 to 8.

**Rivals.** Rival 1 ended near the measured time (1012 for 1011.2) by luck: a VectorE that passes its work on was seen in the old order, but its picture, VectorE as the bound, was not. VectorE idles 55 us in the stage and is busy 85%, where I had named over 92% as the sign. Rival 2: seven of the 96 subtractions lasted over 0.7 us (717 to 945 ns), each while a PARTITION_ALL_REDUCE of GpSimd ran, as did the pass of 954 ns in the kernel before; they are too few for 12.7. Rival 3: the loads do cost half of its 7.7, but hardly by the way it named, since only 2.3 us of VectorE's idle time ahead of the copies were ended by a load. None of them was what decided; all three assumed that TensorE's 12.4 us are first gained and then lost. That no gain was there to lose was no case of mine, and the order as a cause of several us either way was none.

**What I said would show it.** 120 instructions fewer, later parts of the same length: both seen. A copy of 320 columns in 0.4 us from start to start: 0.43. A stage 9 us shorter with 4 to 8 us of idle time: refuted, 6.3 longer with 13.3. Of the signs of being wrong none came clearly: the waits for VectorE listed above make 8.2 us, where I had set 10. The sign that did settle it, the turns left out with no gain, was not among mine.
